# Attention and a low-rank mixer on one core: first weights, first mixing and first layers in another order

## The chip, the core and the metric

The kernel runs on one core of one Trainium2 chip. The metric is the device time of one execution in microseconds; lower is better. Engines are named as in the profile: PE is TensorE (PEld its weight loads), DVE is VectorE, ACT is ScalarE, POOL is GpSimd, SP is SyncE.

## What is computed

For each of 8 batches and 8 heads, attention over 576 tokens with 16 extra beacon keys that every query sees; then a mixer on the 512 concatenated channels:

```
k_all, v_all = concat(beacon_k, k), concat(beacon_v, v)       # 16 + 576 keys, head size 64
a = softmax(causal(q @ k_all^T / 8));   x = a @ v_all         # x as (batch, token, 512)
h = x^T @ U @ V                                               # low rank 32 over the tokens
u = x + h^T
out = u + relu(u @ w_ch1) @ w_ch2                             # 512 -> 2048 -> 512
```

Inputs and output are float32; the kernel computes in float16 with float32 sums in PSUM.

## The kernel before, in words

All instructions of the five engines stand in the order in which the program emits them (a manual schedule), and each engine works through its own in that order. So what an engine does next is set by the place of a call in the source, not by a scheduler.

**Attention** goes by pairs of heads: 4 pairs to a batch, 32 pairs in all (p = 4 x batch + c). The steps of a pair:
- *regroup*: two copies (L220) on VectorE that bring k and q of the pair from the load tile `st` into `pr` (for batch 0, `group_first` spreads these and the casts over three engines);
- *transposes* (L229, L231): TensorE turns q, then k, into a PSUM tile `tps`; VectorE copies each half out in two instructions (L232, L233), 64 or 80 columns and 512 columns. From batch 3 on DMA transposes replace these (L253, L260);
- *scores* (L286), in two visits of two groups for the two heads, into PSUM tiles `sps`; ScalarE takes the exponentials (L292), eight instructions to a pair, into `expt`;
- *masks* (L273, L275): VectorE takes a minimum against the mask for each head, after that head's exponentials;
- *values* (L310): weights times values for each head into `po`, then a reciprocal (L318) and a product into `xb` (L319) on VectorE.

**Mixing** of a batch (`mix_units`): a head (L339) that multiplies `xb` of all four pairs with U, a copy of the result (L345, `qts`), and two parts (L354, L364) that add x and h in PSUM; ScalarE and VectorE copy the result to `uT` (L374, L372).

**The two layers** go by blocks of 512 tokens, 9 in all. A block is 16 first-layer units (L397, four matmuls into `gps`, then a relu into `gT` on ScalarE, L401, or VectorE, L403) and 16 second-layer units (L413, four matmuls into `cps`; the fourth of four also adds u, copies out and stores the result, L421 to L431). Block 0 needs the mixing of batch 0, block 1 that of batches 0 and 1.

**The order.** Mixings and layer units wait in a list called `queue`. `fill(n)` emits the next n of it; `mix(b)` puts the mixing of batch b ahead in the queue, spread among units that are there already, and `feed` appends the units of the blocks that become possible. In the loop over pairs 0 to 7, a turn emits the second visit of scores of pair p+1, the masks and values of pair p, and between the two heads' values the transposes of pair p+2, then the first visit of its scores. `FIRST` says how many queued units are spread over a turn: none for the first four turns, then 10, 5, 4 and 4. After pair 7 `AHEAD` units follow at once. `IDLE` is a number of warm-up matmuls (L211) ahead of scores. Pairs 8 to 31 run in a loop of their own.

**Loads.** Batch 0 comes through SP's and ACT's queues as float32. The rest goes through GpSimd's queue, cast on the way: batch 0's v, then batch 1's k and q in two halves of the heads (pairs 4 and 5, pairs 6 and 7), its v, the weights w1 (in two halves of the columns) and w2, then batch by batch. Each of GpSimd's transfers waits, in the program, for the one eight before it. PSUM is a ring of 8 buffers with one tag: a tile waits for the release of the eighth before it.

Of the kernel before, what the change touches and what calls it, by code (L numbers as in the profile page):

```python
# [17 lines left out]
P = 128  # L18
# [9 lines left out]
def kernel(  # L28
# [13 lines left out]
    nc = tc.nc  # L42
# [6 lines left out]
    NDC = FF // P  # L49
# [49 lines left out]
    def pst(shape, dtype, name):  # L99
        return psum.tile(shape, dtype, tag="ps", name=name)  # L100
# [45 lines left out]
    def emit_w1(i):  # L146
        w1r = moe_w_ch1.rearrange("(cc p) f -> p cc f", p=P)
        fs = ds(FF // 2 * i, FF // 2)
        nc.gpsimd.dma_start(out=w1[:, :, fs], in_=w1r[:, :, fs])
# [12 lines left out]
    def beacon_load(eng, src, dst, hs):  # L162
        eng.dma_start(out=dst[0:Nb], in_=src[hs].rearrange("h p d -> p h d"))  # L163
# [4 lines left out]
    def v_loads(src, bsrc, vs, hs):  # L168
        dst = vs[:, :].rearrange("p (c h e) -> p c h e", h=H, e=E)[:, :, hs, 0:D]
        beacon_load(nc.gpsimd, bsrc, dst[:, 0, :, :], hs)  # L170
        for j in range(NT):
            a = Nb if j == 0 else 0
            nc.gpsimd.dma_start(  # L173
                out=dst[a : a + nq[j], j, :, :], in_=src[hs, ds(q0[j], nq[j]), :].rearrange("h p d -> p h d")
            )
# [12 lines left out]
    def k_loads(b, L, hs):  # L188
        main_load(nc.gpsimd, k[b], L[1][0][:, hs, :], hs)
        head_load(nc.gpsimd, k[b], L[0][0][:, hs, :], hs, Nb)  # L190
# [29 lines left out]
        copy(out=t, in_=by_token(L[1][i][:, 2 * c : 2 * c + 2, :]))  # L220
        return t

    def qkT_units(L, pr, qT, kT, c):

        hs = ds(2 * c, 2)

        def one(i, dst, w):
            ps = pst([P, SK], F16, name="tps")
            nc.tensor.transpose(ps[:, 0:NL], L[0][i][:NL, hs, :], ident[:NL, :NL])  # L229
            for j in range(4):  # L230
                nc.tensor.transpose(ps[:, ds(NL + P * j, P)], pr[i][:, j, :, :], ident)  # L231
            nc.vector.tensor_copy(out=dst[:, c, 0 : w - 4 * P], in_=ps[:, 0 : w - 4 * P])  # L232
            nc.vector.tensor_copy(  # L233
                out=dst[:, c, w - 4 * P : w].rearrange("x (p j) -> x p j", j=4),
                in_=ps[:, NL:SK].rearrange("x (j p) -> x p j", j=4),
            )

        return [lambda: one(1, qT, S), lambda: one(0, kT, SK)]
# [227 lines left out]
    def load_batch(b):  # L466
        Ls[b] = qk_tiles()
        emit_loads(b, Ls[b], vss[b % 2])
# [35 lines left out]
    def group_first(c, i, copy):  # L504

        prs.setdefault(c, []).append(regroup(Ls[0], c, i, copy))
        hs = SETS[c]
        copy(out=Ls[0][0][i][:NL, hs, :], in_=raw["head"][:NL, i, hs, :])

    def regroup_of(p):  # L510
        b, c = divmod(p, NH2)
        prs[p] = [regroup(Ls[b], c, i, nc.vector.tensor_copy) for i in range(2)]
# [24 lines left out]
    def qkT_of(p):  # L537
        b, c = divmod(p, NH2)
        new_qT_of(p)
        if p in raw_of:  # L540
            return order_units(raw_of[p], qTs[b], kTs[b % 2], c)
        return qkT_units(Ls[b], prs[p], qTs[b], kTs[b % 2], c)

    def scores_of(p):
        b, c = divmod(p, NH2)
# [2 lines left out]
    def av_of(p):  # L548
        b, c = divmod(p, NH2)
        if c == 0:  # L550
            xbs[b] = xbp.tile([P, NT, DM], F16, name="xb", tag="xb")
        return [
            lambda i=i: av_unit(b, 2 * c + i, expts[(2 * p + i) % NE], vss[b % 2], xbs[b]) for i in range(2)
        ]


    NF = 2
    HB = 3
    AHEAD = 16
    LAG = 12  # L560
    HINT = 5

    FIRST = [0, 0, 0, 0, 10, 5, 4, 4]

    QUOTA = {2: 4}

# [35 lines left out]
    with tc.manual_schedule(engines={ENG.PE, ENG.Activation, ENG.DVE, ENG.SP, ENG.Pool}):  # L602
        load_first()
        v_loads(v[0], beacon_v[0], vss[0], HALVES[0])
        cast_small = small_loads()
        for i in range(NE):

            nc.vector.memset(expts[i][:, SLOT + gw[1] : 2 * SLOT], 0.0)
            nc.vector.memset(expts[i][:, 3 * SLOT + gw[3] : blk[(3, 4)] + P], 0.0)
        V, G = nc.vector.tensor_copy, nc.gpsimd.tensor_copy  # L610
        group_first(0, 0, act_copy)
        group_first(0, 1, V)
        keep_warm(pst([P, 512], F32, name="idle"), IDLE[0])
        t0, sc = qkT_of(0), scores_of(0)
        for u in t0:
            u()
        sc[0](IDLE[1])
        sc[1]()
        masks = sc[2]
        group_first(1, 0, G)  # L620
        group_first(1, 1, V)
        v_loads(v[0], beacon_v[0], vss[0], HALVES[1])
        for u in qkT_of(1):
            u()
        sc = scores_of(1)
        sc[0](IDLE[2])
        group_first(2, 0, G)

        Ls[1] = qk_tiles()
        group_first(3, 0, G)  # L630
        k_loads(1, Ls[1], HALVES[0])
        q_loads(1, Ls[1], HALVES[0])
        beacon_load(nc.gpsimd, beacon_k[1], Ls[1][0][0], ALLH)
        k_loads(1, Ls[1], HALVES[1])
        q_loads(1, Ls[1], HALVES[1])
        v_loads(v[1], beacon_v[1], vss[1], HALVES[0])
        emit_w1(0)
        emit_w1(1)
        cast_small()
        v_loads(v[1], beacon_v[1], vss[1], HALVES[1])  # L640
        emit_w2()

        NP1 = NF * NH2
        for p in range(NP1):
            b, c = divmod(p, NH2)
            if c == 0 and NF <= b + 1:
                load_batch(b + 1)
            seq = [masks]
            if p + 1 < NP1:
                seq.insert(0, sc[1])  # L650
                masks = sc[2]
            av, qk, sc = av_of(p), [], []
            if p + 2 < NP1:
                if p == 0:
                    seq.append(lambda: group_first(2, 1, V))
                elif p > 1:
                    seq.append(lambda p=p: regroup_of(p + 2))
                qk = [lambda i=i, p=p: qkT_of(p + 2)[i]() for i in range(2)]
            seq += av[0:1] + qk + av[1:2]
            if p + 2 < NP1:  # L660
                new_qT_of(p + 2)
                sc = scores_of(p + 2)
                if p == 0:
                    seq.append(lambda: group_first(3, 1, act_copy))
                seq.append(lambda sc=sc, p=p: sc[0](IDLE[3] if p < NH2 else 0))
            done = 0
            for i, u in enumerate(seq):
                u()
                want = FIRST[p] * (i + 1) // len(seq)
                fill(want - done)  # L670
                done = want
            if c == NH2 - 1:
                mix(b)

        fill(AHEAD)
        regroup_of(NP1)
        regroup_of(NP1 + 1)
        t0, sc, t1 = qkT_of(NP1), scores_of(NP1), qkT_of(NP1 + 1)
        for u in t0 + sc[0:1] + t1[0:1] + sc[1:3] + t1[1:2]:
            u()  # L680
            fill(1)
        for p in range(NP1, NP):
            b, c = divmod(p, NH2)
            if c == 0 and b + 1 < B:
                if b + 1 not in Ls:
                    Ls[b + 1] = qk_tiles()
                    qk_loads(b + 1, Ls[b + 1])
                v_loads(v[b + 1], beacon_v[b + 1], vss[(b + 1) % 2], ALLH)
            if c == 1 and b + 2 < B:
                Ls[b + 2] = qk_tiles()  # L690
                qk_loads(b + 2, Ls[b + 2])
            sc = scores_of(p + 1) if p + 1 < NP else []
            qk = []
            if p + 3 < NP and p + 3 >= HB * NH2:
                turn_of(p + 3)
            if p + 2 < NP:
                if p + 2 < HB * NH2:
                    regroup_of(p + 2)
                qk = qkT_of(p + 2)
            av = av_of(p)  # L700
            if c == 0 and b > NF:
                mix(b - 1)
            seq = sc[0:1] + av[0:1] + qk[0:1] + sc[1:3] + qk[1:2] + av[1:2]
            quota = QUOTA.get(b, 9)
            done = 0
            for i, u in enumerate(seq):
                u()
                want = quota * (i + 1) // len(seq)
                fill(want - done)
                done = want  # L710
        mix(B - 1)
        guard()


        queue.insert(len(queue) - 22, guard_sum)
        fill(len(queue) - 12)
        n_bad = nc.values_load(badi[0:1, 0:1], min_val=0, max_val=P)
        fill(len(queue) - HINT)
        with tc.block():
            tc.mark_branch_hint_location("general", engines=[ENG.PE, ENG.Activation, ENG.DVE, ENG.SP, ENG.Pool])  # L720
            fill(len(queue))
# [95 lines left out]
```

## Time and profile before

| | us |
|---|---|
| median of 3 runs (lowest to highest) | 368.65 (365.96 to 369.41) |
| the profiled execution | 367.15 |
| its span | 365.5 |
| TensorE busy | 349.8 (96%) |
| VectorE, ScalarE, GpSimd busy | 204.7, 173.7, 83.9 |
| granted TensorE clock, mean | 0.994 |

The span is what the trace covers; the execution's own time has 1.65 us more around it. A profile line that begins with two numbers gives a start in us from the span's start and a duration; then come engine, source line, operation, what it writes and reads, sizes and a count; in brackets stands the engine's idle time before it and what ended it. The rows of a window give its length and then the busy time of each engine, the granted clock, the DMA share and GB/s.

### The profile page before, as it was taken

The numbers are of one execution on the slowest core, as the hardware profiler recorded it, in microseconds if no ns is written. First come the engines' busy times: TensorE is split into PE (matmuls) and PEld (weight loads), VectorE is DVE, ScalarE is ACT, GpSimd is POOL, SyncE is SP. The second block draws the span as 40 slices with busy tenths as digits, with TensorE's granted clock in tenths as the row PEclk, the third lists the DMA queues.
The fourth block names the chain that finished last, engine by engine and source line by source line (L and its number), as shares of the span: only waits on it lengthen the run. The fifth ranks groups of instructions, "written<-read, shape, count | busy, mean of one in ns | idle before, by whom it ended". The sixth has DMA issues, their size and how long they took to land.

```text
span 365.5 us, 7721 instructions
## 1 busy us (share of the span) xinstructions
PE 349.8 (96%) x3040; PEld 173.5 (47%) x3040; DVE 204.7 (56%) x565; ACT 173.7 (48%) x382; POOL 83.9 (23%) x123
## 2 busy tenths in 40 slices
PE   7777999999999999999999999999999999999995
PEld 3544545545545444544445444544454555444442
DVE  4887664357776675565666666756566446223311
ACT  3976660177654553466436643674356503401300
POOL 8976436400336001800081005000000000000000
PEclk9989999999999999999999999999999999999999
DMA  9999999990999952999299917942141013013112
GB/s 178 212 151 184 194 201 156 176 170 10 145 136 163 178 80 59 121 190 137 60 111 206 131 35 101 150 74 41 63 120 26 2 57 103 14 59 87 31 44 79
DMA packets 117916, 40.52 MB, mean 111 GB/s; under 512 B 93680, under 2 KB 112112, under 8 KB 117872
## 3 DMA queue, kind: packets, MB, share of 16 engines
q0 software_dynamic: 65904, 17.54, 54.4%
q1 hardware_dynamic: 51520, 22.12, 31.0%
q8 instruction: 25, 0.41, 0.5%
q10 hardware_dynamic: 448, 0.30, 0.3%
q14 instruction: 19, 0.16, 0.1%
HBM read 37.86 MB, written 9.44 MB: 129 GB/s over the span
## 4 chain that ended last, share of the span: by engine, by line
PE 85%; DMA 6%; DVE 3%; ACT 2%; POOL 2%; issue 0%; DVEq 0%; POOLq 0%
PE cps L413 34%; PE gps L397 33%; PE po L310 6%; PE sps L286 6%; DMA w<-in_moe_w_ch_dram 2%; DMA raw<-pr 2%; PE ups L354 2%; DMA st<-in_q_dram 2%; ACT expt L292 2%; PE idle L211 1%; POOL vs L173 1%; DVE gT L403 1%; PE ups L364 1%; PE qtp L339 1%; PE tps L231 1%; DVE expt L273 1%
## 5 line engine op out<-in xcount | busy, mean ns | idle before, releaser
L292 ACT ACTIVATE expt<-sps 128x496 f16<-128x496 f32 (+2 forms) x256 | 111.1, 531 | 61.9 <-PE sps L286 61.7
L397 PE MATMUL gps<-uT,w 128*128 128x512 f16 x576 | 135.7, 379 | 1.8 <-ACT uT L374 1.2
L413 PE MATMUL cps<-w,gT 128*128 128x512 f16 x576 | 134.4, 379 | 0.0
L401 ACT ACTIVATE gT<-gps 128x512 f16<-128x512 f32 x86 | 51.8, 608 | 64.3 <-PE gps L397 62.0
L413 PEld LDWEIGHTS <-gT 128*128 128x128 f16 x576 | 52.3, 98 | 61.1 <-issue 3.7
L397 PEld LDWEIGHTS <-w 128*128 128x128 f16 x576 | 51.8, 98 | 60.8 <-issue 6.1
L403 DVE TENSOR_SCALAR gT<-gps 128x512 f16<-128x512 f32 x58 | 40.1, 691 | 45.7 <-PE gps L397 44.0
L426 DVE TENSOR_TENSOR ob<-cps,ut 128x512 f32<-128x512 f32 x32 | 22.1, 691 | 49.6 <-PE cps L413 49.1
L173 POOL DMA_DIRECT2D vs<-in_v_dram x50 | 40.8, 831 | 14.3 <-DMA st<-in_q_dram 4.9
L310 PEld LDWEIGHTS <-expt 128*128 128x128 f16 (+1 forms) x960 | 36.9, 98 | 15.0 <-DVE expt L273 2.2
L310 PE MATMUL po<-vs,expt 128*128 128x65 f16 (+1 forms) x960 | 40.3, 195 | 1.0 <-DVE expt L273 0.5
L286 PE MATMUL sps<-qT,kT 64*128 64x80 f16 (+4 forms) x384 | 33.4, 286 | 4.0 <-DVE kT L233 3.4
L319 DVE TENSOR_TENSOR xb<-po,rec 128x320 f16<-128x320 f32 x64 | 31.4, 491 | 2.2
L374 ACT ACTIVATE uT<-ups 128x240 f16<-128x240 f32 (+1 forms) x32 | 11.5, 416 | 39.3 <-PE ups L364 39.2
L273 DVE TENSOR_TENSOR expt<-expt,bigmask 128x512 f16<-128x512 f16 x64 | 26.7, 418 | 6.0 <-ACT expt L292 5.9
L163 POOL DMA_DIRECT2D vs<-in_beacon_v_dram x10 | 5.4, 538 | 100.6 <-PE po L310 100.3
L318 DVE RECIPROCAL rec<-po 128x5 f32<-128x5 f32 x64 | 12.0, 187 | 27.0 <-PE po L310 26.2
L286 PEld LDWEIGHTS <-kT 64*128 64x128 f16 x384 | 12.3, 95 | 30.1 <-issue 10.8
L372 DVE CAST uT<-ups 128x240 f16<-128x240 f32 (+1 forms) x32 | 13.1, 450 | 8.5 <-PE ups L364 8.5
L220 DVE COPY pr<-st 128x512 f16<-128x512 f16 x56 | 14.2, 296 | 1.0 <-DMA st<-in_q_dram 0.6
L260 DVE COPY qT<-raw 128x512 f16<-128x512 f16 x20 | 12.4, 619 | 2.7 <-DMA raw<-pr 2.7
L275 DVE TENSOR_TENSOR expt<-expt,mask 80x80 f16<-80x80 f16 x64 | 12.5, 196 | 0.0
(65 smaller groups left out, 157.2 us busy)
## 6 DMA issues: line engine op xcount, KB each, us to landing
out_dram<-ob SPq DMA_DIRECT2D x36, 256.0 KB, 2.3
w<-in_moe_w_ch_dram POOLq DMA_DIRECT2D x4, 1024.0 KB, 11.5
st<-in_k_dram POOLq DMA_DIRECT2D x6, 512.0 KB, 10.0
st<-in_q_dram POOLq DMA_DIRECT2D x6, 512.0 KB, 13.4
vs<-in_v_dram POOLq DMA_DIRECT2D x18, 128.0 KB, 7.5
stm<-in_k_dram SPq DMA_DIRECT2D x4, 256.0 KB, 4.6
vs<-in_v_dram POOLq DMA_DIRECT2D x12, 64.0 KB, 6.2
stm<-in_q_dram SPq DMA_DIRECT2D x3, 256.0 KB, 5.7
```

What stands on the lines that cost most here:

```text
L173: nc.gpsimd.dma_start(out=dst[a : a + nq[j], j, :, :], in_=src[hs, ds(q0[j], nq[j]), :].rearrange("h p d -> p h d"))
L220: copy(out=t, in_=by_token(L[1][i][:, 2 * c : 2 * c + 2, :]))
L273: nc.vector.tensor_tensor(out=e4, in0=e4, in1=bigmask, op=ALU.min)
L286: nc.tensor.matmul(ps[g, i][:, ds(o, w)], kT[hp, c, ds(P * ch, P)], qT[hp, c, ds(qa, w)], start=True, stop=True,)
L292: nc.scalar.activation(out=ex[i][:, ds(SLOT * g, gw[g])], in_=ps[g, i][:, 0 : gw[g]], func=AF.Exp, scale=scale)
L310: nc.tensor.matmul(po[:, j, :], ex[0 : nk[c], ds(blk[(c, j)], P)], vs[0 : nk[c], ds(c * H * E + h * E, E)], start=(c == 0), stop=(c == j),)
L319: nc.vector.tensor_tensor(out=xb[:, :, ds(h * D, D)], in0=po[:, :, 0:D], in1=r.broadcast_to([P, NT, D]), op=ALU.mult)
L397: nc.tensor.matmul(g[:, 0:n], w1[:, cc, ts(dc, P)], uT[:, cc, ds(t0, n)], start=(cc == 0), stop=(cc == NCC - 1))
L401: nc.scalar.activation(out=gT["t"][:, dc, 0:n], in_=g[:, 0:n], func=AF.Relu)
L403: nc.vector.tensor_scalar_max(out=gT["t"][:, dc, 0:n], in0=g[:, 0:n], scalar1=0.0)
L413: nc.tensor.matmul(ps[:m, :], gT["t"][:, dc, ds(P * i, m)], w2[:, dc, :], start=(dc == 0), stop=turned and dc == NDC - 1, skip_group_check ...
L426: nc.vector.tensor_tensor(out=ob[:m, :], in0=ps[:m, :], in1=gT["u"][:m, i, :], op=ALU.add)
```

## The change

It has four parts:
1. The copies of pair 0's turned k go to ScalarE; those of q stay on VectorE.
2. On GpSimd's queue, w1's first half, the casts of U and V, the first half of batch 1's v and w1's second half stand ahead of the loads of k and q for pairs 6 and 7.
3. The loop over pairs 0 to 7 is written out. Pairs 0 to 2 keep their turns. Pair 3's values come one after the other, and batch 0's mixing with the first unit of block 0 follows at once, ahead of pair 5 (the sixth). Then pair 5's regrouping, transposes and scores with units between them, the values of pairs 4 and 5, five units; pair 6 and then pair 7 whole, from regrouping to masks, with a unit after each transpose; then the values of pairs 6 and 7.
4. The sixteen second-layer units of block 0, which in before are partly done by then, are taken out of the queue and put behind block 1's sixteen first-layer units. `AHEAD` is 20 instead of 16, so that batch 1's mixing, block 1's first layer and one unit of block 0's second layer follow pair 7 without anything between them.

```diff
+    def qkT_units(L, pr, qT, kT, c, copies=(None, None)):
...
+            copy = copies[i] or nc.vector.tensor_copy
...
-            nc.vector.tensor_copy(out=dst[:, c, 0 : w - 4 * P], in_=ps[:, 0 : w - 4 * P])
-            nc.vector.tensor_copy(
+            copy(out=dst[:, c, 0 : w - 4 * P], in_=ps[:, 0 : w - 4 * P])
+            copy(
...
-        return qkT_units(Ls[b], prs[p], qTs[b], kTs[b % 2], c)
+        return qkT_units(Ls[b], prs[p], qTs[b], kTs[b % 2], c, (act_copy, None) if p == 0 else (None, None))
...
-    AHEAD = 16
+    AHEAD = 20
...
-    FIRST = [0, 0, 0, 0, 10, 5, 4, 4]
...
         beacon_load(nc.gpsimd, beacon_k[1], Ls[1][0][0], ALLH)
+        emit_w1(0)
+        cast_small()
+        v_loads(v[1], beacon_v[1], vss[1], HALVES[0])
+        emit_w1(1)
         k_loads(1, Ls[1], HALVES[1])
         q_loads(1, Ls[1], HALVES[1])
-        v_loads(v[1], beacon_v[1], vss[1], HALVES[0])
-        emit_w1(0)
-        emit_w1(1)
-        cast_small()
         v_loads(v[1], beacon_v[1], vss[1], HALVES[1])
         emit_w2()
...
-        for p in range(NP1):
...
-            done = 0
-            for i, u in enumerate(seq):
+        def run(us, n):
+            for u in us:
                 u()
-                want = FIRST[p] * (i + 1) // len(seq)
-                fill(want - done)
-                done = want
-            if c == NH2 - 1:
-                mix(b)
+                fill(n)
+
+        def turned_of(p):
+            return [lambda i=i: qkT_of(p)[i]() for i in range(2)]
+
+        for p in range(NH2 - 1):
...
+            run(seq, 0)
+            sc = scores_of(p + 2)
+            sc[0](IDLE[3])
+        run([sc[1], masks] + av_of(NH2 - 1), 0)
+        mix(0)
+        load_batch(2)
+        masks = sc[2]
+        fill(4)
+        regroup_of(5)
+        run(turned_of(5), 1)
+        run([masks], 2)
+        sc = scores_of(5)
+        run(sc[0:2], 1)
+        run(av_of(4) + sc[2:3] + av_of(5), 0)
+        fill(5)
+        for p in (6, 7):
+            regroup_of(p)
+            run(turned_of(p), 1)
+            sc = scores_of(p)
+            run(sc[0:3], 0)
+        run(av_of(6) + av_of(7), 0)
+        second = queue[:]
+        del queue[:]
+        mix(1)
+        queue[3 + NDC : 3 + NDC] = second
 
         fill(AHEAD)
```

## The prediction

> **What bounds the kernel now.** I read the page's first two parts, then the chain that ended last, then the timelines of TensorE, ScalarE and VectorE from 20 to 75 us, then windows of 3.4 us.
>
> ```profile
> PE 349.8 (96%) x3040; PEld 173.5 (47%) x3040; DVE 204.7 (56%) x565; ACT 173.7 (48%) x382; POOL 83.9 (23%) x123
> ...
> PE   7777999999999999999999999999999999999995
> ```
>
> TensorE is the bound, and only the first four slices (36 us) have room. The change adds no matmul, so its worth is the change in TensorE's idle time and clock. Between pair 4 and the first unit of block 1's first layer TensorE is idle 50.59 - 47.99 = 2.60 us, then 0.98 us up to 110:
>
> ```profile
> 22.65:73.24 50.59, 47.99 (x498) 26.18 (x499) 29.28 (x88) 22.77 (x53) 28.54 (x41) 0.97 1.61 176
> 73.24:110.00 36.76, 35.78 (x366) 17.76 (x365) 26.25 (x79) 25.19 (x55) 7.99 (x11) 1.00 1.05 117
> ```
>
> (Columns: length, busy of PE, PEld, DVE, ACT, POOL, granted clock, DMA share, GB/s.) TensorE's waits in that stretch, and the rows that set the pace of one pair of heads on ScalarE and VectorE:
>
> ```profile
> 22.65 0.21 PE L229 MATMUL tps<-ident,hd 80*128 80x80 f16 x1 [1.56 <-DMA hd<-in_q_dram]
> ...
> 29.37 0.89 PE L286 MATMUL sps<-qT,kT 64*128 64x496 f16 x12 [0.79 <-DVE kT L233]
> ...
> 34.93 1.90 PE L397 MATMUL gps<-uT,w 128*128 128x512 f16 x8 [0.58 <-DMA w<-in_moe_w_ch_dram]
> ...
> 52.15 0.62 PE L310 MATMUL po<-vs,expt 128*128 128x65 f16 x15 [0.26 <-DVE expt L273]
> ```
> ```profile
> 25.38 3.38 ACT L292 ACTIVATE expt<-sps 128x496 f16<-128x496 f32 x8 [2.16 <-PE sps L286]
> 29.79 3.38 ACT L292 ACTIVATE expt<-sps 128x496 f16<-128x496 f32 x8 [1.03 <-PE sps L286]
> ```
> ```profile
> 26.10 0.48 DVE L220 COPY pr<-st 128x512 f16<-128x512 f16 x2
> 27.20 0.19 DVE L318 RECIPROCAL rec<-po 128x5 f32<-128x5 f32 x1 [0.62 <-PE po L310]
> 27.43 0.49 DVE L319 TENSOR_TENSOR xb<-po,rec 128x320 f16<-128x320 f32 x1
> ```
>
> A pair needs eight exponentials on ScalarE (3.38 us), which begin about 0.45 us after its scores do, and then VectorE's minima (0.45 per head). That is over 4 us from scores to weights times values. Before hides it: in its loop the scores of pair p+1, the values of pair p and the transposes of pair p+2 alternate, with units of the queue between.
>
> The clock:
>
> ```profile
> 16.68:20.09 3.41, 2.95 (x54) 1.96 (x53) 3.09 (x11) 2.92 (x8) 2.85 (x5) 1.00 1.43 184
> 20.09:23.51 3.42, 1.69 (x44) 1.49 (x39) 2.40 (x10) 3.13 (x8) 2.05 (x4) 1.00 1.60 184
> 23.51:26.92 3.41, 3.41 (x38) 1.72 (x34) 3.04 (x11) 1.54 (x4) 3.41 (x6) 0.50 1.42 106
> ```
>
> After a stretch of 3.4 us in which TensorE was busy 49%, the next 3.4 us ran at half clock. Stretches that were busy 68% or more were not followed by one.
>
> **Part 1, kT of pair 0 copied by ScalarE.** In before VectorE does both transposed halves, 0.70 us each; with ScalarE on the other half the first scores may come about 0.5 us earlier (ScalarE's form for this is not in the trace; the nearest rows are its 0.60 relu and 0.31 for 80x128, together 0.9, so 0.3 to 0.5). I take 0: pair 4's transposes wait until 22.65 for a load that GpSimd issued at 16.22, behind a queue without a gap since 2.3; an earlier front only lengthens that wait of 1.56. Bounds -0.5 (wholly passed on) to +0.3.
>
> **Part 2, order of the loads.** GpSimd's queue takes w1's first half at 17.4 instead of 26.16; the casts of U and V, batch 1's first v half and w1's second half follow; k and q of pairs 6 and 7 come last, and their first transfer waits for w1's first half to land (in the program each of GpSimd's transfers waits for the one eight before it). In before the first half took 8.73 us from issue to landing, much of it queued behind v. Put behind the q load that lands at 22.6 it needs some 5 to 7 us: landed by 28 to 30, before its first use, which I put at 31.7. What is behind: v (3 us at the 100 GB/s of 24 to 28 us) by 32, w1's second half (6 us) by 38, k and q (0.6 MB, 3.3 us) by 41 to 42. Pair 6 is regrouped at about 47.7 in the walk below. So I cost the order at 0, with 6 us of cover; the wait of 0.58 on w1 goes. w2 and batch 2 keep their places.
>
> **Part 3, the new order of pairs 3 to 7**, walked with these rows: first-layer unit 0.87, values of a head 0.47, a transposed half 0.25, scores 0.55 + 0.41, mixing head 0.40, its parts 0.66 and 0.87; VectorE: reciprocal and product 0.62, relu 0.60, regrouping 0.50, one half's copies 0.70, evacuation of a part 0.75 to 0.9. Bold numbers are idle time of TensorE.
> - The values of pair 3 end at 27.5. Mixing's first step needs the last product on VectorE: 27.9 + 0.62 = 28.55. **1.1** idle (before put pair 5's transposes and scores there). The parts run 28.6 to 30.55, without before's three waits for PSUM behind pair 5's exponentials (0.56). Unit 0 waits for the evacuation: 31.7, **1.15**.
> - Pair 5's regrouping stands on VectorE behind the relu of unit 0 (32.8 to 33.4), so its first transpose comes at 34.0: **1.4**.
> - Units 1 to 6, scores and the values of pair 4 run to 41.9 (0.15 on PSUM). The values of pair 5 wait for its exponentials (the second visit's begin behind two relus of ScalarE) and on VectorE for relu 6 and two products: 43.5, **1.6** more. Units 7 to 11 follow to 48.8, pair 6's transposes and units 12, 13 to 51.0, kT **0.35**, scores to 52.35.
> - Here is the largest stall. The minima of pair 6 stand on VectorE ahead of pair 7's regrouping, and behind pair 6's scores TensorE's next instruction is pair 7's first transpose. Scores begin 51.35; exponentials 51.95 to 55.35; minima to 55.85; regrouping to 56.35; transpose 56.4: **4.05**.
> - Two transposes, two units and the scores of pair 7 to 59.7 (0.3 on PSUM). Values of pair 6 to 60.9. Minima of pair 7 (exponentials 59.1 to 62.5) stand ahead of all four products on VectorE: the values of pair 7 start at 62.15 and, for the second head, 63.0: **1.25** and **0.4**. Products end 63.0 + 4 x 0.62 = 65.5; the mixing's head waits for them, **2.05**; its parts end at 67.5; block 1's first unit waits for the evacuation to 68.65, **1.15**. Before covers this mixing with block 0's second layer, which now stands behind block 1's first.
>
> Idle in after 14.95. Removed: 2.60 and the two warm-up matmuls of pair 5 (0.6). Difference +11.7. Second way: before starts block 1's first unit at 73.24 with block 0's sixteen second-layer units done (64 x 0.2155 + 4 x 0.22 = 14.7); without them 58.5, against 68.65: +10.1. The two differ by small gaps between kinds of matmul that the walk lacks. I take +11.
>
> **Part 4, second layer of block 0 beside pairs 8 to 11.** Fifteen first-layer units (an evacuation each) leave that stretch for as many second-layer units (one in four). At best the 0.98 us idle there goes; I take -0.5, bounds -1.0 and 0. The number of queued units is the same from pair 12 on, so nothing moves after that.
>
> **Part 5, the clock.** If a stretch busy about half is followed by 3.4 us at half clock, the idle of 30.5 to 34 (2.5 of 3.45), of 52.35 to 56.4, and of 60.9 to 68.65 (4.85 of 7.75) each bring one or two such stretches. Each costs up to 1.7 us where work follows, less where the next stall absorbs it. Bounds 0 and 6; I take +3.
>
> The Trainium skill ("TensorE: Matmul & The Clock Gate", the practical limits and "HAM oscillation") says that the clock falls back after an idle window of some 3.4 us, so gaps over about 3 us are to be avoided. This trace is stricter: its longest gap before the half clock is 1.56 us. By the page alone only the 4.05 us gap counts and the sum would be about 2 us lower.
>
> **Sum.** 0 + 0 + 11 - 0.5 + 3 = +13.5. The profiled execution took 367.15 (span 365.5); it is 1.5 below the median of the runs, 368.65. So 380.7 beside that execution and 382 for the median.
>
> **Rivals.**
> - *The clock stays full* (0.20): idle as walked, no half-clock stretches: 368.65 + 10.5 = 379. For it: windows are free-running and a stall may be split over two. Against: two windows share the 4.05 us, so one of them is idle at least 2.0 of 3.4. The Trainium skill's rule above would come near this case.
> - *Smaller stalls* (0.12): neighbouring work overlaps more than the walk has it, only the chains of pairs 6 and 7 count (4.05 + 1.25 + 2.05 + 1.15 - 3.2 = 5.3): 374. Against: each step starts on a named row.
> - *The late k and q loads decide* (0.08): if everything behind w1 moved at 100 GB/s, they land at 51 instead of 41, pair 6's regrouping slips by 3.3 us: 385. Against: w and k, q moved at about 200 in before.
> - *The head start stands* (0.05, not slower): the mixing starts at 28.6 instead of 30.42 and the first layer at 31.7 instead of 34.93; if pair 7's transposes followed the scores of pair 6 directly and the queue's units covered the rest, before's 3.2 us would go: 365.5. It decides only if the added idle stays under 3.2 us; it needs VectorE's regrouping ahead of the minima, and the order there is the reverse. The edit that does nothing would be a milder form: 368.
>
> The forecast itself gets 0.55. A measurement of this kernel tells about 1% from no change: faster 0.03, same 0.03, slower 0.94. The range takes the bounds of parts 1, 3, 4 and 5, from 374 (smaller stalls) to 388 (11.7 + 0.3 + 6 + the median's 368.65, and a little over it); some 2 in 10 are left out.
>
> **What would show it.** In the changed kernel's timeline, a wait of about 4 us ahead of a transpose (tps) that names VectorE's pr or expt, near 52 to 56 us; waits of 1 to 2 us ahead of both mixings' qtp, ahead of the first gps of each block, and ahead of po for pairs 5 and 7; granted clock 0.5 in one or more windows between 33 and 72; no wait of GpSimd's k and q loads on the path; busy time from 110 us on shifted, not changed. If the transposes of pair 7 follow the scores of pair 6 within 1 us, or TensorE's idle time between pair 4's transposes and block 1's first unit is under 8 us, the prediction is wrong.

## The result and the profile after

The changed kernel is slower: 381.33 us (median of 4 runs, 379.94 to 382.19) against 368.65 (3 runs, 365.96 to 369.41), 12.7 us more. The ratio, of the means, is 1.0358, with a 95% interval from 1.0282 to 1.0435. A fourth run of before, 372.03 us, lies over 1.5% above its fastest, counts as a slow one and is not in the ratio. The changed kernel's profiled execution took 379.94 us with a span of 378.2.

TensorE's busy time is 353.0 us where before had 349.8: the same matmuls less two warm-ups, more of them at half clock. So of the 12.7 us between the two spans (378.2 and 365.5) 3.2 are busy time and 9.5 are idle time. From the page of the changed kernel:

```profile
PE   7768856999999999999999999999999999999995
...
PEclk9999988699999999999999999999999999999999
```

PEclk is the granted clock. The slices (9.5 us each) from 38 to 66 us stand at 8, 5 and 6 tenths where before had 9s, and the clock row has a dent from 47 to 76 us. A stretch by the side of the one that was shown of before (length, then busy PE, PEld, DVE, ACT, POOL, clock, DMA, GB/s):

```profile
22.65:69.00 46.35, 34.38 (x411) 19.94 (x408) 26.16 (x79) 21.90 (x50) 27.02 (x37) 0.92 1.61 174
...
122.00:378.20 256.20, 250.66 (x2019) 120.92 (x2018) 134.90 (x338) 109.75 (x238) 27.54 (x35) 1.00 0.65 91
```

11.97 us of idle (12.50 up to 69.68, where block 1's first unit starts) stand where before had 2.60, at a mean clock of 0.92. From 122 us on nothing but the place has changed: before is busy 250.86 us in its last 256.20. TensorE's timeline shows where; in brackets is the idle time and what ended it:

```profile
27.43 0.44 PE L340 MATMUL qtp<-xb,Usb 112*32 112x128 f16 x17 [0.80 <-DVE xb L320]
...
30.12 1.02 PE L398 MATMUL gps<-uT,w 128*128 128x512 f16 x4 [0.53 <-ACT uT L375]
...
32.49 0.40 PE L232 MATMUL tps<-ident,pr 128*128 128x128 f16 x4 [1.30 <-DVE pr L220]
...
41.83 1.09 PE L311 MATMUL po<-vs,expt 128*128 128x65 f16 x30 [1.44 <-DVE expt L274]
...
54.69 0.53 PE L232 MATMUL tps<-ident,pr 128*128 128x128 f16 x4 [3.58 <-DVE pr L220]
...
62.28 1.35 PE L311 MATMUL po<-vs,expt 128*128 128x65 f16 x30 [1.48 <-ACT expt L293]
...
65.60 0.69 PE L340 MATMUL qtp<-xb,Usb 112*32 112x128 f16 x17 [1.03 <-DVE xb L320]
69.68 15.04 PE L398 MATMUL gps<-uT,w 128*128 128x512 f16 x64 [0.53 <-ACT uT L375]
```

From the transposes on, the line numbers are one higher than in before. The wait of 3.58 us is the chain of pair 6. ScalarE and VectorE show it as one piece after the other:

```profile
50.27 3.39 ACT L293 ACTIVATE expt<-sps 128x496 f16<-128x496 f32 x8
```
```profile
53.69 0.42 DVE L274 TENSOR_TENSOR expt<-expt,bigmask 128x512 f16<-128x512 f16 x1 [0.18 <-ACT expt L293]
54.03 0.19 DVE L276 TENSOR_TENSOR expt<-expt,mask 80x80 f16<-80x80 f16 x1
54.15 0.48 DVE L220 COPY pr<-st 128x512 f16<-128x512 f16 x2
```

TensorE's wait names the copy (L220), but the copy took 0.48 us. What was late is the exponentials, and the copy of pair 7, which needs none of them, stood behind pair 6's minima in VectorE's order.

The clock, in windows of 3.4 us of the same execution:

```profile
51.40:54.81 3.41, 0.12 (x2) 0.13 (x3) 1.47 (x6) 2.26 (x6) 0.88 (x1) 1.00 1.54 193
54.81:58.23 3.42, 3.42 (x16) 1.76 (x15) 1.56 (x4) 0.60 (x1) 1.75 (x2) 0.50 1.79 179
58.23:61.64 3.41, 2.57 (x45) 1.42 (x42) 0.72 (x2) 2.55 (x7) 2.37 (x4) 1.00 3.39 138
61.64:65.05 3.41, 1.65 (x33) 1.21 (x34) 2.94 (x11) 0.84 (x3) 2.83 (x5) 1.00 1.98 146
65.05:68.47 3.42, 2.87 (x40) 2.28 (x40) 1.50 (x4) 0.63 (x2) 2.90 (x4) 0.50 1.57 188
68.47:71.88 3.41, 2.88 (x14) 1.09 (x12) 0.92 (x2) 1.04 (x3) 1.05 (x2) 0.50 2.99 144
```

Three half-clock windows: one behind the large stall, two behind the waits of pair 7. The other three executions had mean clocks of 0.973, 0.975 and 0.978 where this one has 0.986. A window at half clock takes 3.41 x 0.5 / 378 = 0.0045 off the mean, so they had some two or three windows more.

### The profile page after: what moved, and what is told of

The parts are those of the page before. It is cut to its first block, busy times and chain, and to the rows that moved or that the text cites. A ratio compares the mean times of both kernels' runs of the same rounds, so it can differ in the third digit from the quotient of the medians.

```text
span 378.2 us, 7716 instructions
## 1 busy us (share of the span) xinstructions
PE 353.0 (93%) x3038; PEld 175.5 (46%) x3038; DVE 205.6 (54%) x563; ACT 175.4 (46%) x384; POOL 83.5 (22%) x123
## 4 chain that ended last, share of the span: by engine, by line
PE 84%; DVE 5%; DMA 4%; ACT 3%; POOL 2%; issue 1%; SPq 0%; ACTq 0%
PE gps L398 34%; PE cps L414 32%; PE sps L287 6%; PE po L311 6%; PE ups L355 2%; ACT expt L293 2%; DMA st<-in_q_dram 2%; DVE xb L320 1%; DMA raw<-pr 1%; DMA stm<-in_k_dram 1%; PE ups L365 1%; POOL vs L173 1%; PE tps L232 1%; PE qtp L340 1%; DVE gT L404 1%
## 5 line engine op out<-in xcount | busy, mean ns | idle before, releaser
L398 PEld LDWEIGHTS <-w 128*128 128x128 f16 x576 | 53.7, 99 | 65.8 <-issue 9.2
L311 PEld LDWEIGHTS <-expt 128*128 128x128 f16 (+1 forms) x960 | 36.0, 97 | 16.6 <-DVE expt L274 4.2
L311 PE MATMUL po<-vs,expt 128*128 128x65 f16 (+1 forms) x960 | 39.2, 194 | 3.8 <-ACT expt L293 2.0
L261 DVE COPY qT<-raw 128x512 f16<-128x512 f16 x20 | 12.7, 637 | 4.0 <-DMA raw<-pr 4.0
L232 PE MATMUL tps<-ident,pr 128*128 128x128 f16 x96 | 9.7, 232 | 5.2 <-DVE pr L220 5.2
L220 DVE COPY pr<-st 128x512 f16<-128x512 f16 x56 | 14.1, 294 | 0.7 <-DMA st<-in_q_dram 0.7
```

The source lines that it names most:

```text
L311: nc.tensor.matmul(po[:, j, :], ex[0 : nk[c], ds(blk[(c, j)], P)], vs[0 : nk[c], ds(c * H * E + h * E, E)], start=(c == 0), stop=(c == j),)
L398: nc.tensor.matmul(g[:, 0:n], w1[:, cc, ts(dc, P)], uT[:, cc, ds(t0, n)], start=(cc == 0), stop=(cc == NCC - 1))
```

## The experiments

Ratios are to the kernel before, run on the same chip, with 95% intervals; the changed kernel's own is 1.0358 (1.0282 to 1.0435).

**1. Pair 7's regrouping and transposes ahead of pair 6's masks.**

```diff
-            run(sc[0:3], 0)          # pair 6, masks included
+        run(sc6[0:2], 0)
+        regroup_of(7)
+        run(turned_of(7), 1)
+        sc = scores_of(7)
+        run(sc6[2:3] + sc[0:3], 0)
```

> The changed kernel with pair 7's regrouping and transposes emitted ahead of pair 6's masks (minima) instead of behind them. Theory of the order: the 3.58 us that TensorE waits for VectorE's pr at 51 to 54.7 us goes, ScalarE then takes pair 7's exponentials directly behind pair 6's, and block 1's first unit starts some 5 us earlier (64 to 65 us instead of 69.7): 376 us. Rival, the loads: TensorE is held back by late k and q of pairs 6 and 7, then nothing moves: 381. Rival, the stall only moves on to the next wait on pair 7's masks: 380 or more.

375.55 us, ratio 1.0191 (1.0132 to 1.025): 6 us gained by moving two copies and a pair's transposes (with two queued units) past four minima. TensorE's timeline of this kernel:

```profile
57.65 1.35 PE L311 MATMUL po<-vs,expt 128*128 128x65 f16 x30 [1.48 <-ACT expt L293]
...
64.30 16.29 PE L398 MATMUL gps<-uT,w 128*128 128x512 f16 x64 [0.53 <-ACT uT L375]
```

The 3.58 us are gone, the later waits are as long as they were, and block 1's first unit starts at 64.30 instead of 69.68. So the stall is caused by the order on VectorE; neither of the rivals (loads, a stall that only moves on) holds. The gain is more than the 3.58 us because the half-clock window behind that wait (54.81 to 58.23 in the changed kernel) is gone as well; two half-clock windows remain in this trace, from 62.18 to 69.01.

**2. Warm-up matmuls in the waits.**

```diff
+        keep_warm(pst([P, 512], F32, name="idle"), 3)    # ahead of mix(0)
...
+        keep_warm(pst([P, 512], F32, name="idle"), 4)    # ahead of turned_of(5)
...
+        keep_warm(pst([P, 512], F32, name="idle"), 5)    # ahead of av_of(5)
...
+                keep_warm(pst([P, 512], F32, name="idle"), 14)    # behind pair 6's scores
...
+        keep_warm(pst([P, 512], F32, name="idle"), 5)    # ahead of av_of(7)
...
+        keep_warm(pst([P, 512], F32, name="idle"), 8)    # ahead of mix(1)
```

> The changed kernel with warm-up matmuls (identity times identity, result unused) put into its six long waits of TensorE: 3 ahead of the first mixing, 4 ahead of pair 5's transposes, 5 ahead of pair 5's values, 14 ahead of pair 7's transposes, 5 and 8 around pair 7's values. Nothing else moves. Theory of the clock: the three half-clock stretches of the profile (10.2 us, some 5 of cost) come from the waits and go; 376 to 377, clock 0.995 or more. If idle time alone decides, 381 as before; if the warm-up matmuls are in the way, 382 or more.

375.06 us, ratio 1.0181 (1.0126 to 1.0237), mean clocks of 0.994 to 0.998. The waits are all still there, only filled, and behind 15 us no window of its trace is at half clock until the last matmuls are done:

```profile
54.81:58.23 3.42, 3.06 (x28) 1.60 (x29) 2.52 (x7) 0.85 (x2) 1.47 (x2) 1.00 1.68 185
```
```profile
51.37 3.18 PE L211 MATMUL idle<-ident 128*128 128x512 f16 x14 [0.17 <-ACT expt L293]
55.15 0.40 PE L232 MATMUL tps<-ident,pr 128*128 128x128 f16 x4 [0.56 <-DVE pr L220]
...
67.19 13.97 PE L398 MATMUL gps<-uT,w 128*128 128x512 f16 x64 [0.53 <-ACT uT L375]
```

3.18 + 0.56 is the old 3.58 and a little, and none of the path's work is gone. Yet the time falls by 1.0358 - 1.0181 = 0.0177, or 6.5 us; with the two intervals taken together this is 3 to 10 us. What is left above before, 1.0181, is 6.7 us (4.6 to 8.7) for the waits themselves. The two profiled executions put it otherwise: 378.2 - 374.5 = 3.7 us for the clock, and 374.5 - 365.5 = 9.0 us for the waits, at a mean clock of 0.994 in this one and in before's alike. So the lower clock that the waits brought on is shown, at some 4 to 6 us; its exact share is not.

**3. Block 0's second layer where it was.**

```diff
-        second = queue[:]
-        del queue[:]
         mix(1)
-        queue[3 + NDC : 3 + NDC] = second
...
-    AHEAD = 20
+    AHEAD = 16
```

> The changed kernel with part 4 undone: block 0's second-layer units stay where they are in the queue, three of them after batch 1's mixing head and three after each part, and 16 units follow pair 7. Theory of the order: the wait for the evacuation ahead of block 1's first unit (0.5 us) and a part of the half clock go, the wait for the products ahead of the mixing (1.6 us) stays: 379 to 381. If the placement of the second layer were the main cause: 373 or less. If the second layer's later place was a gain beside pairs 8 to 11: 382.

378.61 us, ratio 1.027 (1.0199 to 1.0341). It points to 3 us, a little more than the 379 to 381 expected, but the interval overlaps that of the changed kernel, so that part 4 cost time is not shown. The wait ahead of the mixing is unchanged here (0.56 and 1.03 us in its trace); the one ahead of block 1's first unit is gone.

**4. and 5. The order of the loads**, undone in the changed kernel (4) and done alone in before (5):

```diff
+        emit_w1(0)
+        cast_small()
+        v_loads(v[1], beacon_v[1], vss[1], HALVES[0])
+        emit_w1(1)
         k_loads(1, Ls[1], HALVES[1])
         q_loads(1, Ls[1], HALVES[1])
...
```

> The changed kernel with part 2 undone: the loads in the order of before. If the order of the loads is worth nothing: 381. If the early first layer needs the early w1: w1's first half lands near 35 us instead of 28, the first unit waits some 4 to 5 us longer, and the time is 384 to 386. If the late k and q of pairs 6 and 7 had cost time: 379 or less.

> The kernel before with part 2 alone: the changed order of the loads. If the order is worth nothing: 369. If k and q of pairs 6 and 7, which before regroups on VectorE at 33 us, land at 36 to 37 instead: VectorE is held some 3 us with the mixing's evacuation behind it, and the first unit starts at 37 to 38 instead of 34.9: 371 to 372. If the early w1 is a gain by itself: 368.

(4) is slower than the changed kernel: 387.1 us, ratio 1.0512 (1.0454 to 1.0571). (5) is slower than before: 372.03 us, ratio 1.013 (1.0088 to 1.0172). TensorE in (4), then VectorE in (5):

```profile
34.64 1.89 PE L398 MATMUL gps<-uT,w 128*128 128x512 f16 x4 [3.69 <-DMA w<-in_moe_w_ch_dram]
```
```profile
36.24 0.29 DVE L220 COPY pr<-st 128x512 f16<-128x512 f16 x1 [3.57 <-DMA st<-in_k_dram]
37.80 0.29 DVE L220 COPY pr<-st 128x512 f16<-128x512 f16 x1 [1.26 <-DMA st<-in_q_dram]
38.01 0.92 DVE L372 CAST uT<-ups 128x336 f16<-128x336 f32 x2
```

In (4) the mixing ends at 31 and the first unit waits 3.69 us for w1; its trace has half clock from 33.20 to 43.44, and the time lies a little above the 384 to 386 expected. In (5) VectorE waits 3.57 and 1.26 us for pair 6's k and q, with the evacuation of the mixing behind it, and the first unit waits 4.38. The queue carries the same bytes either way; each order of pairs needs its own order of loads. Part 2 is a condition of part 3.

**6. ScalarE's copy alone, in before.**

```diff
+        return qkT_units(Ls[b], prs[p], qTs[b], kTs[b % 2], c, (act_copy, None) if p == 0 else (None, None))
```

> The kernel before with part 1 alone: pair 0's turned k copied by ScalarE. The prediction's step: the front comes up to 0.5 us earlier and the wait for batch 1's loads ahead of pair 4 takes it back: no change, 369. Rival: the gain is passed on, 368.3. Rival: ScalarE's copy is slower and delays the exponentials: 369.5.

366.78 us, ratio 0.9995 (0.9976 to 1.0013): no change that can be told from none. The front does move, as its trace shows: the first scores start at 7.64 us, 8.12 in before. Whether the loads take these 0.5 us back is not shown: they are 0.14%, within the interval, and in this trace pair 4's transposes (22.31 instead of 22.65) and the first unit (33.95 instead of 34.93, waiting 0.65 us for w1) still come earlier.

**7. The pairs interleaved again**, with the early mixing, the loads and ScalarE's copy kept. Part 4 is undone in it too, and three warm-up matmuls stand ahead of pair 4's transposes:

```diff
-    AHEAD = 20
+    AHEAD = 13
...
+                seq.append(lambda: keep_warm(pst([P, 512], F32, name="idle"), 3))
...
+        run([sc[1], masks, lambda: regroup_of(5)] + av3[0:1] + turned_of(5) + av3[1:2], 0)
...
         mix(0)
...
+        run([sc[0], sc[1], av[0], av[1]], 1)          # scores of 5, values of 4
+        fill(2)
+        sc[2]()
+        run(av_of(5), 1)
...
         run(sc[0:2], 1)                               # scores of 6
+        regroup_of(7)
+        run(turned_of(7), 1)
+        sc7 = scores_of(7)
+        sc[2]()
+        run(sc7[0:2], 1)
+        run(av_of(6), 1)
+        fill(1)
+        sc7[2]()
+        run(av_of(7), 1)
+        fill(2)
         mix(1)
-        queue[3 + NDC : 3 + NDC] = second
```

> The changed kernel with its pairs interleaved again: early mixing, loads and ScalarE's copy stay, but pair 5's transposes go between pair 3's values, pair 7's ahead of pair 6's masks, a queued unit stands behind every step of pairs 5 to 7, second-layer units stand ahead of batch 1's mixing, and 3 warm-up matmuls ahead of pair 4's transposes. Theory of the order: the early mixing is no loss by itself, only the cover was lost; TensorE is without gaps from some 30 us on, and the time falls to before's or under it: 365 to 369. If the early mixing or the loads were the cause: 375 or more. A wait for w2's second half, which lands near 53 us, may cost 1.

365.71 us (10 runs, 364.7 to 366.61) against 367.23 for before on the same chip, ratio 0.9953 (0.993 to 0.9976): the only version here that beats before. With so many parts changed at once it shows that the order costs nothing when it is covered, not what each part gives. Its first unit starts at 31.19 us, where before's starts at 34.93:

```profile
28.50 0.44 PE L340 MATMUL qtp<-xb,Usb 112*32 112x128 f16 x17 [1.34 <-DVE xb L320]
...
31.19 1.02 PE L398 MATMUL gps<-uT,w 128*128 128x512 f16 x4
```

**8. Experiment 7 with pair 5's scores ahead of the mixing**, as in before (the edit is against experiment 7):

```diff
+        sc[0]()
+        sc[1]()
         fill(1)
         masks()
-        fill(2)
-        run([sc[0], sc[1], av[0], av[1]], 1)
+        fill(3)
+        fill(1)
+        run([av[0], av[1]], 1)
```

> The interleaved kernel with one thing put back: pair 5's scores stand ahead of batch 0's mixing, as in the kernel before, instead of behind it. If the early mixing is what the interleaved kernel gains: the three waits for PSUM behind pair 5's exponentials (0.56 us) come back and the first unit starts later, ratio to before 0.998 to 1.000. If the early mixing is worth nothing (its 1.34 us wait for the last product goes, since the scores fill it): 0.995 as the interleaved kernel, 365.5.

367.19 us (12 runs), ratio 1.0035 (1.0007 to 1.0063). The 1.34 us wait is gone, the three waits for PSUM are back (0.21, 0.18 and 0.17 in its trace), and pair 6's transposes come at 43.43 instead of 41.48. So the early mixing is a gain in an order that covers it: the two ratios come from different chips, but their intervals lie apart. Its size is less sure: 0.8% (3 us) by the ratios, 1.5 us by the medians. Of the 1.95 us between the traces, 0.93 stood there ahead of the mixing (pair 4's transposes at 22.79 instead of 21.86, behind a load), so the order accounts for about 1 us. Neither expectation held: the kernel came out above before, not level with it, and why is open.

**9. Four warm-up matmuls ahead of pair 4's transposes, in before.**

```diff
+            if p == 2:
+                seq.append(lambda: keep_warm(pst([P, 512], F32, name="idle"), 4))
```

> The kernel before with 4 warm-up matmuls ahead of pair 4's transposes, where TensorE waits about 1.5 us for a load at 21 to 22.6 us, and nothing else. If the half-clock stretch at 23.5 us of the profile before comes from that wait and costs 1.2 us in most executions: 366.2, ratio 0.996 to 0.997, and no granted 0.5 before 300 us. If it is rare or off the path: ratio 1.000.

366.8 us, ratio 1.0013 (0.9985 to 1.0041): no gain, though its trace has no half clock before 365 us. In that trace as in before's, w1 sets the first unit:

```profile
34.95 1.90 PE L397 MATMUL gps<-uT,w 128*128 128x512 f16 x8 [0.59 <-DMA w<-in_moe_w_ch_dram]
```

34.93 with the half clock and a wait of 0.58, 34.95 without it and a wait of 0.59. Here the half clock ahead of a wait for a load cost nothing that was measured. Before's other executions agree: on this chip 11 with a mean clock of 0.998 or more have a median of 366.28 us, 10 with 0.993 to 0.995 one of 366.07; on the chip of experiments 5 to 7 the medians are 366.78 (7) and 367.28 (10).

## Why the prediction was right

The forecast was 382 us, 13.5 more than before, for certain stalls at certain places and for the half clock behind them; 381.33 came out, 12.7 more. The places and the mechanism of the largest stall were right. The sizes were off in two terms, one too large and one too small, so that the sum came this close is in part luck.

| Step | predicted idle, us | measured |
|---|---|---|
| ahead of batch 0's mixing | 1.1 | 0.80 |
| ahead of unit 0 | 1.15 | 0.53 |
| pair 5's transposes | 1.4 | 1.30 |
| pair 5's values | 1.6 | 1.44 |
| kT of pair 6 | 0.35 | 0.36 |
| pair 7's transposes | 4.05 | 0.17 + 3.58 |
| pair 7's values | 1.25 + 0.4 | 1.48 |
| ahead of batch 1's mixing | 2.05 | 0.55 + 1.03 |
| ahead of block 1's first unit | 1.15 | 0.53 |
| sum with small waits | 14.95 | 11.86 |

- **Part 3** (the order): the walk is too large by 3 us (11.86 is the 12.50 from 22.65 to 69.68 less 0.64 ahead of pair 4's scores and pair 3's values, which the walk leaves out). The evacuations were walked as starting when a part of the mixing ends and as lasting their full time; measured, the first unit waits 0.53 us each time. The head of the mixing starts before the last product has come (its first matmuls run at 26.39 and 63.56), which the walk left out. Against the 3.2 us removed, 12.50 makes +9.3, not the +11 taken.
- **Part 5** (the clock): probably too small. +3 was taken with 0 to 6 as bounds; experiment 2 gives 6.5 (3 to 10) by the ratios and 3.7 by the profiled executions. The changed kernel's profiled execution is the least slowed of its four: the other three had lower clocks.
- Together 11 + 3 stood for about 9.3 + 3.7 in the profiled executions, and for 6.7 + 6.5 by the ratios of experiment 2. Either way the order was put too high and the clock too low, and the two errors offset each other.
- **Part 1** (0): not contradicted; experiment 6 cannot tell 0 from the bound of -0.5. **Part 2** (0): right for the changed kernel, where no wait names k or q of pairs 6 and 7; but experiments 4 and 5 show that this 0 is a balance, -5.7 us (0.0154) for the new loads under the new order and +4.8 us (1.3%) for them under the old.
- **Part 4**: the gain of 0.5 us is not seen. From 69.68 to 122 us the changed kernel is idle 1.13 us, with waits of 0.29 and 0.82; before has 0.98 from 73.24 to 110. The cover that batch 1's mixing lost by part 4 is counted in part 3.
- **The rivals.** *The clock stays full* is what experiment 2 made: 6.7 us above before, where the rival had 10.5. *Smaller stalls* fails by its condition: the waits ahead of batch 0's mixing and in pair 5, which it left out, are all there. *Late k and q* is refuted by the trace. *The head start stands* failed here for the reason given, VectorE's regrouping behind the minima, and experiment 7 is near to that case, with the order put right: 1.5 us under before on its chip, where the rival had 3.2.
- **The page of the Trainium skill** ("TensorE: Matmul & The Clock Gate", "HAM oscillation") ties the half clock to an idle window of about 3.4 us. The window of 51.40 to 54.81, 0.12 us busy, agrees. The one of 61.64 to 65.05 was busy 1.65 of 3.41 and no gap in it was longer than 1.48 us, and half clock followed: here the measurement decides, as it did in the trace of before.

## What to carry to other kernels

An engine that works in order delays the next item's first step behind this item's last one: when a loop is written out by hand, emit the copies and transposes that the next pair needs ahead of the work that waits for this pair's slow engine, and keep queued work for the places where TensorE would wait. A new order of compute and the order of its loads have to be changed together; each alone lost time here, and so did both without the cover. A stall on TensorE can cost more than its own length when its windows of 3.4 us fall to about half busy and work on the path follows: here the half clock added 3.7 us to 9.0 by the traces, 6.5 to 6.7 by the ratios. Ahead of a wait for a load (experiment 9) the same half clock cost nothing.

## What the runs showed of the hardware that was not expected

- In the profile after, windows 61% and 62% busy (20.68 to 24.10: 2.10 us; 30.93 to 34.34: 2.11 us) were not followed by half clock; windows 48 and 49% busy were (61.64 here, 20.09 in before). The busy share alone does not decide it: in experiment 1 the window from 58.77, busy 1.82 us (53%), was followed by half clock and the one from 55.35, busy 1.85 us (54%), was not; nor were, in experiments 3 and 8, windows 49 and 48% busy (30.73 to 34.15: 1.68 us; 8.41 to 11.83: 1.64 us).
- The half-clock window of 65.05 to 68.47 was 84% busy by the profile and was followed by a second one; that of 54.81 to 58.23, 100% busy, was not. Both ran at half clock; what decides there stays open.
- 39 matmuls with an unused result, in waits that they did not shorten, made the kernel 1.7% faster (experiment 2).
